# A new written-out order, masks placed by the plan, and one explicit wait between GpSimd and VectorE, in a two-layer linear-attention and GLU kernel

## The chip, the cores and the metric

The kernel runs on one core of one Trainium2 chip. A time is the device time of one execution in microseconds (us), and a kernel's time is the median of several. Engines are named as the profile names them: PE is TensorE (PEld its weight loads), DVE is VectorE, ACT is ScalarE, POOL is GpSimd, SP is SyncE, which here only issues DMAs. A `q` behind an engine's name means its sequencer. "L588" is line 588 of the kernel before; the changed kernel has lines of its own, and what stood at L588 stands there at L621.

## The reference, cut to what matters

The input `x` has 2048 tokens of 512 features in bfloat16. Four residual blocks follow each other; blocks 1 and 3 share one set of weights, and so do blocks 2 and 4.

```python
def _A_ref(x, wqkv, w_phi, wo):          # H = 32 heads of Dh = 16
    q, k, v = split_heads(x @ wqkv)
    pq, pk = q @ w_phi, k @ w_phi        # per head, 16 x 16
    phi_q = concat([softmax(pq), softmax(-pq)])
    phi_k = concat([softmax(pk), softmax(-pk)])
    kv, z = sum_s phi_k^T v, sum_s phi_k # over all 2048 tokens
    return ((phi_q @ kv) / (phi_q . z + 1e-6)) @ wo

def _B_ref(x, W_gate, W_up, W_down):     # F = 1376
    return (relu(x @ W_gate) * (x @ W_up)) @ W_down

x = x + _A_ref(_layernorm(x), ...)
x = x + _B_ref(_layernorm(x), ...)
x = x + _A_ref(_layernorm(x), ...)
x = x + _B_ref(_layernorm(x), ...)
```

`kv` and `z` are sums over all tokens, so no query of a layer can be finished before the last key of that layer has been added.

## The kernel before, in words

The tokens are 16 tiles of 128, and four tiles make a chunk. One layer is a block A and the block B behind it; there are two layers. The functions below do not issue instructions. Each makes operations with an engine, a function that issues the instructions, and the keys that it reads and writes, and puts them into one list, the plan. `Plan.order` then arranges them by the table `ORDER`, one number for each of the 1881 operations, and `Plan.emit` issues them in that order. Each engine executes its own operations in the order of the table and waits where an input is missing. Which engine does an operation that several could do is written in the strings of `STEP` (A is ACT, D is DVE, P is POOL). The numbers given to `pl.op` (durations, earliest times) take no part in the emitted program: `ORDER` alone decides.

The start of the program matters most here. `setup` issues the loads of `x` and the weights (L162), and clears constants. ACT loads its table with a first activation (L172). PE runs 20 dummy matmuls of 128x512 on zeros (L261, `wake`), until work arrives. Then `feature_weights` transposes the key weights, `wkv`, on PE (L294), copies them out (L250 on ACT, L252 on DVE), and folds the 16x16 feature maps into them (L307). For the folding and for the sums at the end of the keys it needs two small masks, `M8` (L198) and `M4` (L200), which DVE makes in `setup`.

LayerNorm of a tile is `BN_STATS` and `BN_AGGR` on DVE (L331, L333), a reciprocal root on POOL (L341), and a scale on ACT, DVE or POOL (L403, L415). The normalised tile is turned by PE (L424, with a copy by ACT or DVE) or by a transposing DMA from SP.

A key tile then takes: four PE matmuls (L653), two exponentials on ACT (L674), sums of exponentials on DVE (L625, L631, L635; for some tiles POOL adds halves first, L622), a reciprocal on DVE (L683), a scaling of the 1024 columns (L688), of which POOL does a first part and DVE the rest as `STEP["ks0"]` says, and PE's sums into `kv` (L711). Value tiles are L606 and their copies L250 or L252. When all 16 key tiles are in, DVE builds `R` from `kv` (L733). Query tiles (L753, L757, ...) can run ahead of that up to the matmul with `R` (L792); DVE divides (L810, L812), PE projects (L843), and DVE adds to `x` (L509). Block B is `glu`: gate and up matmuls (L556), their evictions (L562, L566) and product (L569, L573), the down projection of eleven matmuls a tile (L588), and DVE's addition to `x` (L513). In the last block SP sends each tile out behind that addition (L593); tile 15 goes in three pieces of 256, 128 and 128 columns.

Of the kernel before, what the change touches and what calls it, by code (L numbers as in the profile page):

```python
# [8 lines left out]
P = 128  # L9
D = 512  # L10
# [7 lines left out]
EPS = 1e-5  # L18
# [7 lines left out]
Alu = mybir.AluOpType  # L26
AF = mybir.ActivationFunctionType
AX = mybir.AxisListType
# [22 lines left out]
class Plan:  # L51
# [53 lines left out]
    def emit(self):  # L105
        for o in self.order():
            for b in sorted(o.bufs, key=lambda b: b.kind):
                if b.tile is None:
                    pool, n = self.kinds[b.kind]
                    b.tile = pool.tile(list(b.shape), b.dtype, name=f"{b.kind}{b.slot}", tag=f"{b.kind}{b.slot}", bufs=1)  # L110
            o.fn()

# [4 lines left out]

NV = 8
# [3 lines left out]
WF_IN, WK_IN, WV_IN, WQ_IN, LOADED = 3.5, 5.95, 10.0, 14.1, 13.0  # L122
X_IN = [3.27, 3.85] + [7.2] * 2 + [8.5] * 4 + [11.4] * 4 + [12.8] * 4
TINY = 0.165
# [7 lines left out]
def setup(ctx, tc, A_x, A_wqkv, A_w_phi, A_wo, B_W_gate, B_W_up, B_W_down, out):  # L132
# [32 lines left out]
    for what in LOAD_ACT:  # L165
        load(nc.scalar, what)
# [5 lines left out]
    nc.scalar.activation(out=wake[:], in_=st.zero[:, 0:1], func=AF.Exp)  # L172
    M8f = const.tile([P, 8], F32, name="M8f")
# [24 lines left out]
    nc.vector.tensor_copy(out=M8[:], in_=M8f[:])  # L198
    st.M4 = const.tile([P, 4], BF16, name="M4")
    nc.vector.tensor_reduce(out=st.M4[:], in_=ident[:].rearrange("p (k h) -> p h k", h=4), axis=AX.X, op=Alu.max)  # L200
# [45 lines left out]
def evacuate(st, eng, ends, on_dve, **deps):  # L246

    nc, pl = st.nc, st.pl
    if eng == "A":
        pl.op("ACT", 0.475, lambda: nc.scalar.copy(out=ends()[0], in_=ends()[1]), **deps)  # L250
    else:
        pl.op("DVE", on_dve, lambda: nc.vector.tensor_copy(out=ends()[0], in_=ends()[1]), **deps)  # L252

# [59 lines left out]
class Norm:  # L313
# [8 lines left out]
    def add(self, t):  # L322
# [5 lines left out]
        if self.sums:  # L328
            return self.add_sums(t, n)
        bn = Buf("bnst", [P, 6], F32)  # L330
        pl.op("DVE", 0.597, dur=0.69, fn=lambda: nc.vector.bn_stats(out=bn[:], in_=st.X[:, t, :]), reads=[("X", t)] + ([("Xin", t)] if self.at else []), writes=[(bn, 0)],  # L331
# [448 lines left out]
def attention(st, c, pT, norm, L):  # L780
# [73 lines left out]
    "turn": "AAADDAAD", "wake": 20, "fuse0": "AFAA", "fuse1": "FFFF", "gate": 3, "sA": 3, "xB0": "ADAADDDADDDAAAAA",  # L854
# [5 lines left out]
}  # L860
ORDER = [int(i) for i in """
# [119 lines left out]
def kernel(  # L981
# [4 lines left out]
    with tc.manual_schedule():  # L986
        st.pl.emit()
# [30 lines left out]
```

## Time and profile before

| what | us |
|---|---|
| median of 3 runs | 378.02 (377.85 to 378.4) |
| the profiled execution | 377.86 |
| its span, first to last instruction | 376.1 |
| PE busy | 368.5 |
| DVE busy | 262.5 |
| ACT busy | 212.5 |
| POOL busy | 136.5 |

The profiled execution lies inside the spread of the runs, 0.16 us under their median. Around its span lie 377.86 - 376.1 = 1.76 us. A timeline row reads: start, time until the end of the last instruction in the row, engine, line, operation, what it writes and reads, how many; in brackets the idle time of the engine ahead of it and what ended it. PE's rows overlap, because matmuls are pipelined, so what a matmul costs is the distance between starts.

### The profile page before, as it was taken

What the parts mean: (1) busy time and instruction counts of PE and PEld (TensorE: products, weight loads), DVE (VectorE), ACT (ScalarE), POOL (GpSimd) and SP (SyncE); (2) the same over time, 40 slices, a digit from 0 to 9 for tenths busy, and PEclk for the clock granted to TensorE, in tenths of its full rate; (3) what the DMA queues carried; (4) which work ended last, traced back from release to release, by engine and by line L of the source; (5) the groups of instructions that cost most, each with busy time, mean ns of one, the idle gap of its engine ahead of it and who ended that gap; (6) DMA issues with size and microseconds to landing.
All of it is one profiled execution on the core that took longest, in us unless ns stands there. A gap on an engine that the chain in (4) does not pass through costs nothing.

```text
span 376.1 us, 6927 instructions
## 1 busy us (share of the span) xinstructions
PE 368.5 (98%) x2530; PEld 196.6 (52%) x2530; DVE 262.5 (70%) x608; ACT 212.5 (57%) x478; POOL 136.5 (36%) x223
## 2 busy tenths in 40 slices
PE   8999998999999999999999999999999999999996
PEld 4455445877644545444444446566655454444453
DVE  7999999998879854267554976898875353325343
ACT  4999898767745537784666264786522352042100
POOL 6999998362410028024601765431410011000000
PEclk9999999999999999999999999999999999999999
DMA  8898565675843823400140032266583321000031
GB/s 267 178 194 186 139 147 99 116 108 120 133 93 63 120 43 71 98 0 2 29 92 7 15 58 44 49 121 127 119 136 84 58 62 24 0 14 2 0 110 60
DMA packets 95746, 31.83 MB, mean 85 GB/s; under 512 B 87424, under 2 KB 95200, under 8 KB 95712
## 3 DMA queue, kind: packets, MB, share of 16 engines
q1 hardware_dynamic: 93024, 27.97, 38.4%
q10 hardware_dynamic: 2688, 3.42, 2.7%
q8 instruction: 20, 0.33, 0.4%
q14 instruction: 14, 0.11, 0.1%
HBM read 8.44 MB, written 2.10 MB: 28 GB/s over the span
## 4 chain that ended last, share of the span: by engine, by line
PE 83%; DVE 12%; ACT 1%; DMA 1%; POOL 1%; issue 1%
PE ps L556 37%; PE ps L588 20%; PE ps L843 7%; PE ps L753 4%; PE ps L653 4%; PE ps L536 3%; PE ps L606 3%; DVE b L688 3%; PE q L792 2%; DVE sk L625 2%; DVE rk L683 2%; PE ps L261 1%; DVE sk L635 1%; DMA b<-b 1%; PE q L711 1%; DVE bnst L331 1%
## 5 line engine op out<-in xcount | busy, mean ns | idle before, releaser
L566 ACT ACTIVATE b<-ps 128x512 bf16<-128x512 f32 (+3 forms) x110 | 50.4, 482 | 68.1 <-PE ps L556 67.8
L556 PE MATMUL ps<-b,wu 128*128 128x512 bf16 (+3 forms) x440 | 82.1, 321 | 0.2 <-ACT sq L491 0.2
L556 PE MATMUL ps<-b,wg 128*128 128x512 bf16 (+3 forms) x440 | 81.5, 321 | 0.0
L588 PE MATMUL ps<-wd,b 128*128 128x512 bf16 (+4 forms) x374 | 79.2, 366 | 0.0
L588 PEld LDWEIGHTS <-b 128*128 128x128 bf16 (+1 forms) x374 | 35.3, 98 | 39.3
L556 PEld LDWEIGHTS <-wg 128*128 128x128 bf16 x440 | 38.5, 98 | 31.6
L556 PEld LDWEIGHTS <-wu 128*128 128x128 bf16 x440 | 38.4, 98 | 31.0 <-issue 0.5
L622 POOL TENSOR_TENSOR b<-b 128x256 f32<-128x256 bf16 x39 | 27.5, 718 | 62.8 <-ACT b L757 33.5
L569 DVE SCALAR_TENSOR_TENSOR b<-ps,b 128x512 bf16<-128x512 f32 (+2 forms) x60 | 34.1, 593 | 22.6 <-PE ps L556 12.2
L757 ACT ACTIVATE b<-ps 128x512 bf16<-128x512 f32 x64 | 37.3, 642 | 8.9 <-PE ps L753 7.6
L674 ACT ACTIVATE b<-ps 128x512 bf16<-128x512 f32 x64 | 37.7, 645 | 5.9 <-PE ps L653 5.4
L688 POOL TENSOR_TENSOR b<-b,rk 128x1024 bf16<-128x1024 bf16 (+6 forms) x26 | 36.7, 1424 | 7.5 <-DVE rk L683 4.4
L513 DVE SCALAR_TENSOR_TENSOR X<-ps,r,X 128x512 bf16<-128x512 f32 (+2 forms) x22 | 14.9, 694 | 27.7 <-PE ps L588 27.7
L653 PE MATMUL ps<-Wk,b 128*128 128x512 bf16 x128 | 32.2, 379 | 0.6 <-ACT b L250 0.3
L843 PE MATMUL ps<-wo,b 128*128 128x512 bf16 x128 | 32.7, 379 | 0.0
L753 PE MATMUL ps<-Wq,b 128*128 128x512 bf16 x128 | 32.0, 379 | 0.0
L606 PE MATMUL ps<-wkv,b 128*128 128x512 bf16 x128 | 31.8, 379 | 0.0
L509 DVE SCALAR_TENSOR_TENSOR X<-ps,X 128x512 bf16<-128x512 f32 x32 | 21.7, 679 | 7.4 <-PE ps L843 7.4
L562 ACT ACTIVATE b<-ps 128x128 bf16<-128x128 f32 (+2 forms) x50 | 20.5, 430 | 8.9 <-PE ps L556 8.4
L573 DVE TENSOR_TENSOR b<-b,b 128x128 bf16<-128x128 bf16 (+2 forms) x50 | 15.0, 332 | 14.8 <-ACT b L562 9.8
L773 POOL TENSOR_TENSOR b<-b,rq 128x512 bf16<-128x512 bf16 x21 | 22.1, 1056 | 0.7
L812 DVE TENSOR_TENSOR b<-q,dd 128x512 bf16<-128x512 f32 x32 | 21.8, 683 | 0.6
(94 smaller groups left out, 482.7 us busy)
## 6 DMA issues: line engine op xcount, KB each, us to landing
out_dram<-X SPq DMA_DIRECT2D x15, 128.0 KB, 1.9
X<-in_A_x_dram ACTq DMA_DIRECT2D x3, 512.0 KB, 6.6
b<-b SPq DMA_TRANSPOSE x91, 3.1
wg<-in_B_W_gate_dram SPq DMA_DIRECT2D x8, 160.0 KB, 2.7
wu<-in_B_W_up_dram SPq DMA_DIRECT2D x8, 160.0 KB, 3.2
wd<-in_B_W_down_dram SPq DMA_DIRECT2D x5, 256.0 KB, 3.2
wkv<-in_A_wqkv_dram ACTq DMA_DIRECT2D x2, 512.0 KB, 5.9
wq<-in_A_wqkv_dram ACTq DMA_DIRECT2D x1, 512.0 KB, 4.0
```

Of the source, the lines that this page charges most:

```text
L556: nc.tensor.matmul(ps[:], lhsT=wt[:, b, f * P:(f + 1) * P], rhs=xnT[:, lo:hi, b, :], start=(b == 0), stop=(b == NDB - 1))
L566: pl.op("ACT", 0.045 + 0.43 * share, lambda ups=ups, ru=ru, sign=1.0 if fuse else -1.0: nc.scalar.activation(out=ru[:], in_=ups[:], func=A ...
L569: pl.op("DVE", 0.058 + 0.548 * share, dur=0.138 + 0.548 * share, fn=lambda gps=gps, ru=ru, h=h, cs=cs: nc.vector.scalar_tensor_tensor(out= ...
L588: nc.tensor.matmul(yps[:], lhsT=hs[f][:fsz, ti * P:(ti + 1) * P], rhs=st.wd[:fsz, f, cols], start=(f == 0), stop=(f == NFT - 1))
L606: nc.tensor.matmul(vp[:], lhsT=xnT[:, ti, kb, :], rhs=st.wkv[:, kb, D:2 * D], start=(kb == 0), stop=(kb == NDB - 1))
L622: nc.gpsimd.tensor_tensor(out=h[:].rearrange("p j h f -> p j f h"), in0=x[:, :, 0], in1=x[:, :, 1], op=Alu.add)
L653: nc.tensor.matmul(ps[:], lhsT=xnT[:, ti, kb, :], rhs=w(kb), start=(kb == 0), stop=(kb == NDB - 1))
L674: pl.op("ACT", 0.48, lambda s=s, ek=ek, pk=pk: nc.scalar.activation(out=ek[:, :, s, :], in_=pk[:].rearrange("p (j x) -> p j x", j=8), func ...
L688: eng.tensor_tensor(out=phiK[:, lo:hi, :, :].rearrange("p j s (f h) -> p (j s) f h", h=4), in0=ek[:, lo:hi, :, :].rearrange("p j s (f h) - ...
L753: nc.tensor.matmul(pq[:], lhsT=xnT[:, ti, kb, :], rhs=st.Wq2[:, kb, :], start=(kb == 0), stop=(kb == NDB - 1))
L757: pl.op("ACT", 0.48, lambda s=s, eq=eq, pq=pq: nc.scalar.activation(out=eq[:, :, s, :], in_=pq[:].rearrange("p (j x) -> p j x", j=8), func ...
L843: nc.tensor.matmul(yps[:], lhsT=turned(b), rhs=st.wo[:, b, :], start=(b == 0), stop=(b == NDB - 1))
```

## The change

The list of operations stays the same but for three things: the two masks are operations of the plan now (`masks`), five instead of four value tiles of layer 1 are copied out by DVE, and these are others (`ev1`). A variant of the statistics that would run on ACT is added but not used (`"st"` holds only D). The table `ORDER` is a new one throughout. Two loads of ACT's queue (`x` of tiles 4 to 7, and the value weights) are issued behind the activation that loads ACT's table. The emitter can add a wait: operation 230, POOL's scale of key tile 3, now waits for operation 195, DVE's scale of key tile 0. The constants `WF_IN` to `X_IN` are earliest times for the plan and not part of the program.

```diff
+    def emit(self, tc):
         for o in self.order():
...
             o.fn()
+            o.ins = tc.nc.cur_bb.bb.instructions[-1]
+            for v in BEHIND.get(o.i, ()):
+                tc.add_manual_dep(o.ins, self.ops[v].ins.name, mybir.DependencyInfo(mybir.DependencyClass.Sync, mybir.DependencyReason.ANTI),
[...]
...
+BEHIND = {230: (195,)}
...
-    for what in LOAD_ACT:
+    for what in LOAD_ACT[:3]:
         load(nc.scalar, what)
...
     nc.scalar.activation(out=wake[:], in_=st.zero[:, 0:1], func=AF.Exp)
+    for what in LOAD_ACT[3:]:
+        load(nc.scalar, what)
...
-    nc.vector.tensor_copy(out=M8[:], in_=M8f[:])
     st.M4 = const.tile([P, 4], BF16, name="M4")
-    nc.vector.tensor_reduce(out=st.M4[:], in_=ident[:].rearrange("p (k h) -> p h k", h=4), axis=AX.X, op=Alu.max)
...
+def masks(st):
+
+    nc, pl = st.nc, st.pl
+    pl.rank("w")
+    pl.op("DVE", 0.1, lambda: nc.vector.tensor_copy(out=st.M8[:], in_=st.M8f[:]), writes=[("M8", 0)], at=2.75)
+    pl.op("DVE", 0.17, lambda: nc.vector.tensor_reduce(
+        out=st.M4[:], in_=st.ident[:].rearrange("p (k h) -> p h k", h=4), axis=AX.X, op=Alu.max), reads=[("M8", 0)], writes=[("M4", 0)], at=2.75)
...
-    "xm1": "21121122", "om0": "12222222", "om1": "21221222", "ev0": "AAAAAAAAAAAAAAAA", "ev1": "DAAAAAADAAAAADAD",
...
+    "ev0": "AAAAAAAAAAAAAAAA", "ev1": "AAADADADAAADDAAA", "ks0": "6087060714860850", "ks1": "3484716308718788",
...
 ORDER = [int(i) for i in """
-3 4 5 108 109 110 111 112 113 114 115 116 117 118 7 6 138 8 134 0 9 12 13 14 15 129 128 139 135 16 130 142 131 140
+3 4 5 6 7 14 15 9 8 10 110 111 112 113 114 115 116 117 140 144 136 118 16 17 18 0 132 11 130 131 141 23 145 137 142
```

What the table moves shows in the order of each engine's instructions. The first place is the start on PE. Before, eleven dummy matmuls on `zero` stand ahead of the first transposition of `wkv`; these are the last three of them:

```order
L261 MATMUL ps_140<-zero 128x512
L261 LDWEIGHTS zero
L261 MATMUL ps_142<-zero 128x512
L261 LDWEIGHTS zero
L261 MATMUL ps_144<-zero 128x512
L294 LDWEIGHTS wkv
L294 MATMUL ps_151<-ident,wkv 128x128
```

In the changed kernel these are the seventh and eighth dummy, and the transpositions (now L310) follow:

```order
L277 MATMUL ps_146<-zero 128x512
L277 LDWEIGHTS zero
L277 MATMUL ps_148<-zero 128x512
L310 LDWEIGHTS wkv
L310 MATMUL ps_151<-ident,wkv 128x128
```

Three dummies have moved from ahead of the transpositions to places among them and the foldings behind them.

The second place is POOL around its scale of key tile 3, 128x896 with `rk` of tile 3 as its factor. Before, it stands between two additions of halves (L622):

```order
L341 TENSOR_TENSOR rstd_599<-ve_577,mhalf 128x2
L391 TENSOR_TENSOR ve_613<-u_581,rstd_579 128x2
L391 TENSOR_TENSOR ve_629<-u_568,rstd_599 128x2
L688 TENSOR_TENSOR b_428<-b_427,rk_611 128x896
L622 TENSOR_TENSOR b_704<-b_587 128x8x8x4
L688 TENSOR_TENSOR b_346<-b_345,rk_521 128x1024
```

In the changed kernel the scale of key tile 2, 128x1024, stands directly behind it, and the 128x896 scale is the instruction that got the explicit wait:

```order
L422 TENSOR_SCALAR u_619<-mv_518 128x2
L424 TENSOR_TENSOR ve_621<-u_619,rstd_617 128x2
L721 TENSOR_TENSOR b_441<-b_440,rk_631 128x896
L721 TENSOR_TENSOR b_346<-b_345,rk_509 128x1024
L424 TENSOR_TENSOR ve_689<-u_614,rstd_583 128x2
L655 TENSOR_TENSOR b_691<-b_572 128x8x8x4
```

An addition and one of the small factors of the statistics have moved behind both scales, so POOL now scales twice in a row.

The third place is the end of DVE's program, its additions to `x` in the last block. Before, the last one is a piece of 256 columns of tile 15:

```order
L513 SCALAR_TENSOR_TENSOR X<-ps_5318,r_4853,X 128x512
L513 SCALAR_TENSOR_TENSOR X<-ps_5287,r_4853,X 128x128
L513 SCALAR_TENSOR_TENSOR X<-ps_5334,r_4851,X 128x512
L513 SCALAR_TENSOR_TENSOR X<-ps_5348,r_4853,X 128x512
L513 SCALAR_TENSOR_TENSOR X<-ps_5362,r_4853,X 128x256
```

In the changed kernel the three pieces come earlier and two whole tiles, 8 and 13, close the program:

```order
L546 SCALAR_TENSOR_TENSOR X<-ps_5318,r_4978,X 128x128
L546 SCALAR_TENSOR_TENSOR X<-ps_5332,r_4978,X 128x128
L546 SCALAR_TENSOR_TENSOR X<-ps_5306,r_4978,X 128x256
L546 SCALAR_TENSOR_TENSOR X<-ps_5344,r_4895,X 128x512
L546 SCALAR_TENSOR_TENSOR X<-ps_5362,r_4978,X 128x512
```

The last addition, and the last transfer out behind it, have grown from 256 to 512 columns.

More of the change, by code (lines that the diff above doesn't have):

```diff
@@ L103, in order @@
         return self.seq
-    def emit(self):
+    def emit(self, tc):
         for o in self.order():
@@ L111, in emit @@
             o.fn()
+            o.ins = tc.nc.cur_bb.bb.instructions[-1]
+            for v in BEHIND.get(o.i, ()):
+                tc.add_manual_dep(o.ins, self.ops[v].ins.name, mybir.DependencyInfo(mybir.DependencyClass.Sync, mybir.DependencyReason.ANTI),
+                                  reason="one at a time on the port that VectorE and GpSimd share")
 class KS:
     pass
+BEHIND = {230: (195,)}
 NV = 8
@@ L121 @@
 LATE = ((8, 12), (12, 16), "q")
-WF_IN, WK_IN, WV_IN, WQ_IN, LOADED = 3.5, 5.95, 10.0, 14.1, 13.0
-X_IN = [3.27, 3.85] + [7.2] * 2 + [8.5] * 4 + [11.4] * 4 + [12.8] * 4
+WF_IN, WK_IN, WV_IN, WQ_IN, LOADED = 3.57, 5.83, 10.1, 14.03, 13.0
+X_IN = [3.35, 4.26] + [6.46] * 2 + [8.61] * 4 + [11.37] * 4 + [12.62] * 4
 TINY = 0.165
@@ L329, in add @@
             return self.add_sums(t, n)
+        by_act = self.at is not None and n == 1 and STEP["st"][t] == "A"
+        if by_act:
+            e2, nv, rstd = Buf("u", [P, 4], F32), Buf("ve", [P, 4], F32), Buf("rstd", [P, 4], F32)
+            for out, func, scale in ((lambda: e2[:, 0:1], AF.Square, D ** -0.5), (lambda: mv[:, 0, 0:1], AF.Identity, 1.0 / D)):
+                junk = Buf("sq", [P, D], BF16)
+                pl.op("ACT", 0.67, lambda out=out, func=func, scale=scale, junk=junk: nc.scalar.activation(
+                    out=junk[:], in_=st.X[:, t, :], func=func, scale=scale, accum_out=out()),
+                    reads=[("X", t), ("Xin", t)], writes=[(junk, 0), (e2, 0) if func == AF.Square else (mv, 0)], at=self.at[t])
+            pl.op("POOL", TINY, lambda: nc.gpsimd.tensor_scalar(
+                out=nv[:, 0:1], in0=mv[:, 0, 0:1], scalar1=mv[:, 0, 0:1], scalar2=e2[:, 0:1], op0=Alu.mult, op1=Alu.subtract),
+                reads=[(mv, 0), (e2, 0)], writes=[(nv, 0)])
+            pl.op("POOL", TINY, lambda: nc.gpsimd.tensor_scalar(
+                out=nv[:, 0:1], in0=nv[:, 0:1], scalar1=-1.0, scalar2=EPS, op0=Alu.mult, op1=Alu.add), reads=[(nv, 0)], writes=[(nv, 0), ("stat", t)])
+            pl.op("POOL", 0.39 + 0.155, lambda: nc.gpsimd.tensor_tensor(out=rstd[:, 0:1], in0=nv[:, 0:1], in1=st.mhalf[:, 0:1], op=Alu.pow),
+                  reads=[(nv, 0)], writes=[(rstd, 0)])
+            self.tiles.append(t)
+            return self.normalise(n, mv, rstd)
         bn = Buf("bnst", [P, 6], F32)
-        pl.op("DVE", 0.597, dur=0.69, fn=lambda: nc.vector.bn_stats(out=bn[:], in_=st.X[:, t, :]), reads=[("X", t)] + ([("Xin", t)] if self.at else []), writes=[(bn, 0)],
+        pl.op("DVE", 0.597, dur=0.69, fn=lambda: nc.vector.bn_stats(out=bn[:], in_=st.X[:, t, :]), reads=[("X", t)] + ([("Xin", t), ("M4", 0)] if self.at else []), writes=[(bn, 0)],
               at=self.at[t] if self.at else 0.0)
@@ L853 @@
     "tB0": "A---", "tB1": "---A", "tA": "----", "wev": "DDDAAAAADDDAAAAA", "xn1": "APAPDAADPAAPAAAA",
-    "turn": "AAADDAAD", "wake": 20, "fuse0": "AFAA", "fuse1": "FFFF", "gate": 3, "sA": 3, "xB0": "ADAADDDADDDAAAAA",
[5 rows of a table removed]
+    "st": "DDDDDDDDDDDDDDDD", "turn": "AAADDAAD", "wake": 20, "fuse0": "AFAA", "fuse1": "FFFF", "gate": 3, "sA": 3,
[6 rows of a table added]
 }
 ORDER = [int(i) for i in """
[72 rows of a table removed]
[72 rows of a table added]
 """.split()]
@@ L939, in layers @@
     load_weights(st)
+    masks(st)
     xA = []
@@ L986 @@
     with tc.manual_schedule():
-        st.pl.emit()
+        st.pl.emit(tc)
 _INS = ['A_x', 'A_wqkv', 'A_w_phi', 'A_wo', 'B_x', 'B_W_gate', 'B_W_up', 'B_W_down']
```

151 rows, old and new, of tables (ORDER, STEP) are left out of this document.

## Prediction

> **What bounds the kernel now.** I read the windows first, a table by stage with the busy time (and instructions) of PE, PEld, DVE, ACT and POOL, then PE's clock, the DMAs' share and GB/s, then PE's own waits, then the timelines of the stages in which PE waits.
>
> ```profile
> 20.00:40.00 20.00, 20.00 (x152) 10.42 (x150) 20.00 (x41) 20.00 (x40) 19.62 (x27) 1.00 0.81 174
> 40.00:58.13 18.13, 16.44 (x142) 8.51 (x139) 18.13 (x34) 15.53 (x31) 16.09 (x18) 1.00 0.57 140
> 58.13:212.00 153.87, 153.26 (x1031) 83.20 (x1030) 112.14 (x284) 99.44 (x244) 52.80 (x98) 1.00 0.41 73
> 212.00:262.00 50.00, 49.28 (x455) 28.51 (x454) 40.68 (x95) 31.77 (x71) 23.80 (x33) 1.00 0.40 75
> 262.00:372.90 110.90, 110.90 (x645) 56.28 (x643) 54.33 (x111) 31.29 (x68) 8.53 (x13) 1.00 0.26 56
> ```
>
> From 58 us on PE is the bound: it waits 0.6 us in 154, 0.7 in 50, nothing in the last 111. Its matmuls are the same in both kernels, so a new order can win or lose there only what PE waits. Ahead of 58.13 it is otherwise. That is the start of `R`, and in the 38 us before it DVE is busy without a break, while PE finds 1.7 us of idle time between 40 and 58.
>
> ```profile
> 58.13 0.77 DVE L733 TENSOR_TENSOR R<-M,q 128x272 bf16<-128x272 bf16 x2
> ```
>
> PE's row behind it waits for just that:
>
> ```profile
> 59.04 0.41 PE L792 MATMUL q<-R,b 128*128 128x68 bf16 x8 [0.29 <-DVE R L733]
> ```
>
> So the time is: the moment at which DVE reaches `R`, then PE's work behind it with 1.3 us of waits, then the tail. In both orders the same matmuls stand on PE ahead of its first L792, and on DVE the same operations ahead of L733. What can move the first term is DVE's idle time ahead of `R` and the length of its instructions.
>
> **The start.** DVE's rows up to 18 us show all its idle time of that stage.
>
> ```profile
> 3.38 0.69 DVE L331 BATCH_NORM_STATS2 bnst<-X 128x6 f32<-128x512 bf16 x1 [0.60 <-DMA X<-in_A_x_dram]
> ...
> 5.12 0.25 DVE L200 TENSOR_REDUCE M<-ident 128x4 bf16<-128x128 bf16 x1
> 5.29 0.16 DVE L198 CAST M<-M8f 128x8 bf16<-128x8 f32 x1
> 5.48 0.76 DVE L270 TENSOR_TENSOR Wblk<-M,wf 128x256 bf16<-128x256 bf16 x2
> 6.58 1.18 DVE L252 COPY b<-ps 128x512 bf16<-128x512 bf16 x3 [0.34 <-PE ps L294]
> ...
> 15.62 0.42 DVE L252 COPY b<-ps 128x512 bf16<-128x512 bf16 x1 [0.28 <-PE ps L424]
> ...
> 17.80 0.42 DVE L252 COPY b<-ps 128x512 bf16<-128x512 bf16 x1 [0.24 <-PE ps L424]
> ```
>
> The masks now come ahead of the first `BN_STATS`, into the 0.60 us in which DVE waits for `x`. They held DVE from 5.12 to 5.48, 0.36 us. But the copy at 6.58 already waits 0.34 for PE, and PE cannot turn `wkv` before it has landed, so that wait grows by the same 0.36: the masks alone give nothing at once.
>
> PE's side changes more.
>
> ```profile
> 1.24 4.88 PE L261 MATMUL ps<-zero 128*128 128x512 bf16 x11 [1.24 <-DVE zero L170]
> 5.91 1.61 PE L294 MATMUL ps<-ident,wkv 128*128 128x128 bf16 x16
> ...
> 7.58 0.59 PE L261 MATMUL ps<-zero 128*128 128x512 bf16 x2
> 8.01 0.83 PE L307 MATMUL ps<-Wblk,b 128*128 128x128 bf16 x12
> ```
>
> ```profile
> 5.86 1.25 PEld L294 LDWEIGHTS <-wkv 128*128 128x128 bf16 x12 [0.66 <-DMA wkv<-in_A_wqkv_dram]
> ```
>
> Eleven dummies take 5.91 - 1.24 = 4.67 us, 0.425 each; two later ones take 8.01 - 7.58 = 0.43, 0.215 each. PE starts at half speed (the PEclk column shows 1.00 throughout and misses this). Sixteen transpositions take 1.44 us; at 0.215 / 4 and twice that a column block costs 0.054 and 0.107, so about eleven were slow and the step came near 5.91 + 11 x 0.107 = 7.1 us, after 5.8 us of unbroken work. With eight dummies PE is done at 1.24 + 8 x 0.425 = 4.64 and idles 1.2 us until `wkv` lands at 5.86. If the idle time does not matter, the step stays at 7.1. If PE must again be busy for 5.8 us, it comes at 11.7. I take 10.5, nearer to the only stretch that the rows show. [...]
>
> With the step at 10.5, 3.4 us more pass at half speed, and PE falls back by 1.7 us. DVE needs PE's turned tiles at the two copies quoted at 15.62 and 17.80, and there it has no slack now. In the new order it has some: tile 3's copy stands behind one more `BN_STATS` (0.59 us to the next start) and PE turns that tile 0.25 earlier, tile 4's turn stands 1.1 earlier on PE and its copy 0.3 earlier on DVE, so both have about 0.8. DVE then stalls 1.7 - 0.8 = 0.9, less the 0.28 + 0.24 that it waits there now: +0.4. ACT starts its exponentials late by as much; the sums of key tile 4 and 6 have under 1 us of slack to them, and I add 0.2. **Head: +0.6 us**. Without the delay both stalls vanish, -0.5; with the step at 11.7 the lag is 2.3 and the head +1.2.
>
> **The scales.** On DVE, the length of an L688 scale depends on what POOL does.
>
> ```profile
> 27.77 0.28 DVE L688 TENSOR_TENSOR b<-b,rk 128x256 bf16<-128x256 bf16 x1
> ...
> 28.75 0.62 DVE L688 TENSOR_TENSOR b<-b,rk 128x1024 bf16<-128x1024 bf16 x1
> ...
> 31.42 2.54 DVE L688 TENSOR_TENSOR b<-b,rk 128x1024 bf16<-128x1024 bf16 x2
> ```
>
> POOL's rows of the same stretch:
>
> ```profile
> 31.04 1.69 POOL L688 TENSOR_TENSOR b<-b,rk 128x896 bf16<-128x896 bf16 x1
> 32.70 1.12 POOL L622 TENSOR_TENSOR b<-b 128x256 f32<-128x256 bf16 x1
> 33.77 1.96 POOL L688 TENSOR_TENSOR b<-b,rk 128x1024 bf16<-128x1024 bf16 x1
> ```
>
> The 1024-wide scale alone takes 0.62 us and the 256-wide one 0.28; the pair begun inside POOL's scale of tile 3 takes 2.54, 1.6 more. So a DVE scale that meets a POOL scale can lose up to what is left of it, 1.7 to 2.0 us. In the new order other pairs meet: the scale of key tile 4 falls where POOL adds, tiles 7, 8 and 9 fall into POOL's scale of tile 7. I find some gained and some lost and take 0, with -1.2 to +1.2 as bounds, about one long collision either way.
>
> **The explicit wait** is for DVE's scales of key tiles 1 and 0, 0.62 + 0.28 us behind the reciprocal for which POOL's scale waits anyway.
>
> ```profile
> 28.30 0.54 DVE L683 RECIPROCAL rk<-sk 128x64 bf16<-128x64 f32 x1
> ```
>
> That reciprocal ends at 28.84 now and POOL starts at 31.04, 2.2 us later, because its own queue holds it; the work ahead of it on POOL stays within 0.2 us. 0.9 fits into 2.2: cost 0, at most 0.9. If POOL came early, the scale of tile 2 (1.96), additions for `sk` and `sq`, and behind them PE's sums L711 would wait too. The table load moved ahead of two loads costs nothing: the row below shows an issue during it.
>
> ```profile
> 3.63 1.28 ACT L172 ACT_TABLE_LOAD   x1 [3.63 <-issue]
> 3.70 0.47 ACTq L162 DMA_DIRECT2D X<-in_A_x_dram  x1
> ```
>
> The last load of `x` is now issued behind an ACT copy of PE's transpositions, some 0.7 us later than the 5.99 of before; its tiles 12 to 15 are first used at 18.14, so this is covered.
>
> **Layer 2's start.** PE waits for a transposition once.
>
> ```profile
> 224.49 1.04 PE L653 MATMUL ps<-Wk,b 128*128 128x512 bf16 x4 [0.23 <-DMA b<-b]
> ```
>
> In the new order the four last down projections of layer 1 follow each other, with the value matmuls behind them, so the chain from the last of them starts 1.9 us of PE work earlier. That can take away this wait and the gap around it, 0.4 us from start to start; DVE has one more copy of a value tile there (0.66), in a stretch in which it is busy 40.7 of 50 us. **I take -0.2**, between -0.4 and a new wait of +0.4.
>
> **The tail.** The last rows of DVE, and the transfers out with the time to their landing:
>
> ```profile
> 372.01 0.75 DVE L513 SCALAR_TENSOR_TENSOR X<-ps,r,X 128x512 bf16<-128x512 f32 x1 [1.63 <-PE ps L588]
> 373.21 0.48 DVE L513 SCALAR_TENSOR_TENSOR X<-ps,r,X 128x256 bf16<-128x256 f32 x1 [0.46 <-PE ps L588]
> ```
>
> ```profile
> out_dram<-X SPq DMA_DIRECT2D x11, 128.0 KB, 1.8
> out_dram<-X SPq DMA_DIRECT2D x2, 32.0 KB, 1.5
> out_dram<-X SPq DMA_DIRECT2D x1, 64.0 KB, 1.5
> ```
>
> PE ends with the same total of work, but what follows its last matmul is an addition over 512 columns instead of 256, 0.75 - 0.48 = 0.27, and a transfer of 128 KB instead of 64 KB, 1.8 - 1.5 = 0.3. Nothing hides the end. **Tail: +0.55 us**, between 0.27 and 0.9 (the slowest landing of a transfer out).
>
> **Sum.** +0.6 + 0 + 0 - 0.2 + 0.55 = +0.95. The profiled execution took 377.86 us with a span of 376.1; it would take 378.8. Put on the median of the runs, which is 0.16 above it, this is 378.02 + 0.95 = **379.0 us**.
>
> **Rivals.** First, the cover holds: the stretch at half speed does not grow, DVE's two stalls go, -0.5, one collision of scales less, -0.6, the wait of layer 2 goes, -0.4; with the tail +0.55 the sum is -0.95, 377.1, and 376.5 at the far bound of the scales, -1.2. For it speaks that PE was busy 3.4 us before its pause, against it that this had not raised its speed. Second, PE's lag is covered but nothing is won: 0 at the head, tail +0.55, layer 2 -0.2, 378.4, within the bound. [...] Last, the explicit wait may do nothing, since it is met before POOL gets there; this holds in every case above, and is why it has no term.
>
> **How the numbers follow.** About 0.2%, 0.76 us, is what a measurement of this kernel can tell from no change. My forecast, 378.2 to 379.8 around 379.0, gets 0.38, of which 0.10 lies within 0.2%. The rival that is faster gets 0.28 (0.22 beyond 0.2%), the covered one 0.16, the collisions 0.18. So faster 0.22, same 0.10 + 0.06 + 0.16 = 0.32, slower 0.28 + 0.18 = 0.46. The range of 376.7 to 381.0 leaves out a third of the first outer case and half of the last, 0.18.
>
> **What would show it.** The start on PE: eight dummies, a pause of 1.2 us, and where the distance of two dummies falls from 0.43 to 0.215 us; at 7.1 my head is wrong. [...] The last addition on DVE should take 0.75. If PE's idle time between 58 and 372 has grown by more than 1 us, I have missed a wait that the new order makes where PE is the bound.

## The result, and the profile after

The changed kernel takes 377.37 us (median of 12 runs, 376.99 to 377.72), the kernel before 378.14 in the same comparison (12 runs). The ratio is 0.998, with an interval of 0.9973 to 0.9988: faster by 0.5 to 1.0 us, where a slower one was forecast. The profiled execution took 377.40 us with a span of 375.7, against 377.86 and 376.1.

Three moments cut the span into the terms of the prediction: PE's first matmul on `R`, DVE's last addition to `x`, and the end. In the changed kernel PE's and DVE's timelines have these rows:

```profile
59.11 0.41 PE L825 MATMUL q<-R,b 128*128 128x68 bf16 x8
```

```profile
372.31 0.75 DVE L546 SCALAR_TENSOR_TENSOR X<-ps,r,X 128x512 bf16<-128x512 f32 x1 [1.63 <-PE ps L621]
```

| stretch | before, us | after, us | measured | forecast |
|---|---|---|---|---|
| head: start to the first matmul on `R` | 59.04 | 59.11 | +0.07 | +0.6 |
| body: from there to the last addition | 373.21 - 59.04 = 314.17 | 372.31 - 59.11 = 313.20 | -0.97 | -0.2 |
| tail: from there to the end of the span | 376.1 - 373.21 = 2.89 | 375.7 - 372.31 = 3.39 | +0.50 | +0.55 |
| sum | | | -0.40 | +0.95 |

**The head** comes out even, but not because nothing happened. DVE's rows of waiting for PE, ahead of the same copies as before, have grown:

```profile
6.60 0.42 DVE L259 COPY b<-ps 128x512 bf16<-128x512 bf16 x1 [0.77 <-PE ps L310]
...
16.84 0.42 DVE L259 COPY b<-ps 128x512 bf16<-128x512 bf16 x1 [0.77 <-PE ps L457]
...
18.36 0.42 DVE L259 COPY b<-ps 128x512 bf16<-128x512 bf16 x1 [0.51 <-PE ps L457]
```

They are 2.05 us now and were 0.34 + 0.28 + 0.24 = 0.86. On PE's timeline the reason is seen:

```profile
5.95 1.46 PE L310 MATMUL ps<-ident,wkv 128*128 128x128 bf16 x12 [1.12 <-DMA wkv<-in_A_wqkv_dram]
7.21 0.63 PE L277 MATMUL ps<-zero 128*128 128x512 bf16 x1
...
9.34 0.63 PE L277 MATMUL ps<-zero 128*128 128x512 bf16 x1
9.77 0.43 PE L323 MATMUL ps<-Wblk,b 128*128 128x128 bf16 x4
10.03 0.38 PE L277 MATMUL ps<-zero 128*128 128x512 bf16 x1
```

The dummies at 7.21 and 9.34 are followed after 0.42 and 0.43 us by the next row, the one at 10.03 after 0.21 (the next row, not shown, starts at 10.24). So the step to full speed fell near 9.8 us, behind the pause, as the forecast had it (10.5). The trace also records when the full clock was granted, here from 9.84 us on.

What paid for this is the second half of the head. The groups of DVE's scales up to 58.13 us, by shape (busy time, then mean ns of one); first before, then after:

```profile
L688 DVE TENSOR_TENSOR b<-b,rk 128x1024 bf16<-128x1024 bf16 x5 | 5.2, 1041 | 0.0
...
L688 DVE TENSOR_TENSOR b<-b,rk 128x128 bf16<-128x128 bf16 x2 | 0.6, 289 | 0.0
```

```profile
L721 DVE TENSOR_TENSOR b<-b,rk 128x1024 bf16<-128x1024 bf16 x5 | 3.3, 654 | 0.0
L721 DVE TENSOR_TENSOR b<-b,rk 128x128 bf16<-128x128 bf16 x2 | 2.2, 1096 | 0.0
```

And all thirteen together, before and after:

```profile
L688 DVE TENSOR_TENSOR b<-b,rk 128x1024 bf16<-128x1024 bf16 (+5 forms) x13 | 10.3, 807 | 0.0
```

```profile
L721 DVE TENSOR_TENSOR b<-b,rk 128x1024 bf16<-128x1024 bf16 (+5 forms) x13 | 8.8, 709 | 0.0
```

The busy times differ by 1.5 us, but records of neighbouring scales overlap in them. Thirteen times the means, and the distances from start to next start, give 1.3 us less. The five wide ones run near the 0.62 us of one that nothing disturbs. The three of 256 columns, of which two began inside additions of POOL before, take 0.75 us less together:

```profile
L688 DVE TENSOR_TENSOR b<-b,rk 128x256 bf16<-128x256 bf16 x3 | 1.8, 594 | 0.0
```

```profile
L721 DVE TENSOR_TENSOR b<-b,rk 128x256 bf16<-128x256 bf16 x3 | 1.0, 345 | 0.0
```

The two small ones of 128 columns now take 0.96 and 1.23 us, 1.6 us more together, because both begin inside a scale of POOL. The first of them, and POOL's two scales:

```profile
31.82 0.96 DVE L721 TENSOR_TENSOR b<-b,rk 128x128 bf16<-128x128 bf16 x1
```

```profile
31.01 3.57 POOL L721 TENSOR_TENSOR b<-b,rk 128x896 bf16<-128x896 bf16 x2
```

**The body.** All that PE waits for between 58 and 372 us, before and after:

```profile
PE ps L832 <- DVE b L812: 0.3, 1, 0.3
PE q L792 <- DVE b L812: 0.3, 1, 0.3
PE q L792 <- DVE R L733: 0.3, 1, 0.3
PE ps L653 <- DMA b<-b: 0.2, 1, 0.2
PE ps L556 <- ACT sq L491: 0.2, 1, 0.2
```

```profile
PE ps L865 <- ACT b L790: 0.3, 1, 0.3
PE q L825 <- DVE b L845: 0.3, 1, 0.3
```

The wait of 0.3 us for `R` lies ahead of the first matmul on `R`, in the head. The two waits of 0.2 us are gone. Counted from start to start of matmuls, less what such a matmul costs elsewhere, they were gaps of 0.39 us near 224 and 0.32 near 253; three of 0.07 to 0.09 us between 68 and 79, which the list is too coarse for, have gone too.

**The tail** did what was said: the last addition takes 0.75 us, and the transfers out of 128 KB in the last stretch need

```profile
out_dram<-X SPq DMA_DIRECT2D x3, 128.0 KB, 1.8
```

1.8 us to land, where the 64 KB piece needed 1.5.

### The profile page after: what moved, and what is told of

It is laid out like the page before. It is cut to its first block, busy times and chain, and to the rows that moved or that the text cites. A ratio compares the mean times of both kernels' runs of the same rounds, so it can differ in the third digit from the quotient of the medians.

```text
span 375.7 us, 6932 instructions
## 1 busy us (share of the span) xinstructions
PE 368.1 (98%) x2530; PEld 197.2 (52%) x2530; DVE 264.0 (70%) x609; ACT 211.4 (56%) x477; POOL 136.4 (36%) x223
## 4 chain that ended last, share of the span: by engine, by line
PE 87%; POOL 6%; DVE 5%; DMA 1%; issue 0%; ACT 0%; ACTq 0%
PE ps L589 37%; PE ps L621 20%; PE ps L876 7%; PE ps L786 5%; PE ps L686 4%; PE ps L639 4%; PE ps L569 3%; PE q L825 2%; POOL b L721 2%; POOL b L655 2%; PE q L744 1%; DMA wkv<-in_A_wqkv_dram 1%; POOL b L448 1%; DVE b L721 1%; DVE rk L716 1%; PE ps L277 1%
## 5 line engine op out<-in xcount | busy, mean ns | idle before, releaser
L621 PE MATMUL ps<-wd,b 128*128 128x512 bf16 (+3 forms) x374 | 79.2, 366 | 0.0
L655 POOL TENSOR_TENSOR b<-b 128x256 f32<-128x256 bf16 x39 | 26.3, 687 | 50.9 <-ACT b L790 31.6
L790 ACT ACTIVATE b<-ps 128x512 bf16<-128x512 f32 x64 | 36.2, 616 | 7.6 <-PE ps L786 5.8
L721 POOL TENSOR_TENSOR b<-b,rk 128x1024 bf16<-128x1024 bf16 (+6 forms) x26 | 37.7, 1461 | 7.0 <-DVE rk L716 7.0
L707 ACT ACTIVATE b<-ps 128x512 bf16<-128x512 f32 x64 | 36.8, 629 | 4.9 <-PE ps L686 4.7
L257 ACT CAST vext<-ps 128x512 bf16<-128x512 f32 x27 | 16.2, 620 | 12.7 <-PE ps L639 12.7
L524 ACT ACTIVATE sq<-b 128x512 bf16<-128x512 bf16 x32 | 20.2, 632 | 4.2 <-DVE b L503 4.1
```

The lines of the kernel that those rows point to most:

```text
L621: nc.tensor.matmul(yps[:], lhsT=hs[f][:fsz, ti * P:(ti + 1) * P], rhs=st.wd[:fsz, f, cols], start=(f == 0), stop=(f == NFT - 1))
L655: nc.gpsimd.tensor_tensor(out=h[:].rearrange("p j h f -> p j f h"), in0=x[:, :, 0], in1=x[:, :, 1], op=Alu.add)
L707: pl.op("ACT", 0.48, lambda s=s, ek=ek, pk=pk: nc.scalar.activation(out=ek[:, :, s, :], in_=pk[:].rearrange("p (j x) -> p j x", j=8), func ...
L721: eng.tensor_tensor(out=phiK[:, lo:hi, :, :].rearrange("p j s (f h) -> p (j s) f h", h=4), in0=ek[:, lo:hi, :, :].rearrange("p j s (f h) - ...
L790: pl.op("ACT", 0.48, lambda s=s, eq=eq, pq=pq: nc.scalar.activation(out=eq[:, :, s, :], in_=pq[:].rearrange("p (j x) -> p j x", j=8), func ...
```

## The experiments

Each was compared with the kernel before on the same chip. Some are hybrids of the two orders, which are easy to make: of the operations ahead of `R` of layer 1 only nine stand on different sides of it in the two tables, and of those ahead of `R` of layer 2 one. Besides the times, the table at the end of this section has the three stretches of every profile.

**1. Without the explicit wait** (`a_nowait`)

```diff
-BEHIND = {230: (195,)}
+BEHIND = {}
```

> The changed kernel without its explicit wait; the order is untouched. Theory (the wait is met before GpSimd gets to the scale of key tile 3): the scale starts at 31.0 us as in the changed kernel, VectorE's R starts within 0.1 us of 58.18, and the time stays about 0.8 us under the kernel before (ratio 0.998). Rival (the wait keeps the two engines' scales apart, and the shorter scales on VectorE, 8.8 instead of 10.3 us in 13, come from it): without it that sum goes back towards 10.3, R comes 1 us or more later, near 59.3, and the time is at or above the kernel before.

Measured: 377.75 us, ratio 0.9991 (0.9982 to 1.0). POOL's timeline shows no idle time ahead of the scale, with the wait gone:

```profile
31.21 0.20 POOL L424 TENSOR_TENSOR ve<-u,rstd 128x2 f32<-128x2 f32 x1
31.36 3.57 POOL L721 TENSOR_TENSOR b<-b,rk 128x896 bf16<-128x896 bf16 x2
```

The thirteen scales take 8.8 us as in the changed kernel, so the rival, which put the shorter scales down to the wait, falls. `R` comes 0.35 us later, and so does POOL's scale; in this profile the step to full speed came at 10.6 us instead of 9.8, and DVE's waits for PE are 2.52 us instead of 2.05. The wait is met when POOL gets there: in the changed kernel DVE's scale of tile 0 ends by 29.99, POOL begins at 31.01. The time itself doesn't settle it: its interval meets that of the changed kernel.

**2. Eleven dummies ahead again** (`a_eleven`), in `ORDER`:

```diff
-110 111 112 113 114 115 116 117 140 144 136 118
+110 111 112 113 114 115 116 117 118 119 120 140 144 136
```

(119 and 120 are taken out where they stood, further on)

> The changed kernel with eleven dummy matmuls ahead of the first transposition, as before, instead of eight. Theory (the pause on PE delays the step to full speed, and the delay costs VectorE): the distance of 512-column matmuls falls to 0.215 us near 7.1 us instead of 9.9; VectorE's waits for PE ahead of its copies shrink from 2.0 us to about 0.9; R starts 0.6 to 0.9 us earlier, near 57.4, and the time is 0.6 to 0.9 us under that of the changed kernel (1.4 to 1.7 under the kernel before). Rival 1 (the speed of PE at the start is covered further on, or the scales fall into each other in another way when VectorE comes earlier): R stays within 0.3 us of 58.18. Rival 2 (the step comes at about 10 us however PE is used before): the rows of the start do not change.

Measured: 377.11 us, ratio 0.9974 (0.9965 to 0.9983). DVE's timeline:

```profile
17.18 0.42 DVE L259 COPY b<-ps 128x512 bf16<-128x512 bf16 x1 [0.20 <-PE ps L457]
...
26.47 0.42 DVE L664 TENSOR_REDUCE sk<-b 128x32 f32<-128x256 f32 x1 [0.58 <-POOL b L655]
...
57.98 0.79 DVE L766 TENSOR_TENSOR R<-M,q 128x272 bf16<-128x272 bf16 x2
```

The step came at 6.0 us and the waits for PE shrank from 2.05 to 1.1 us, as the theory had it, but `R` gained 0.2 and not 0.6 to 0.9, with the first tile of `x` landing at the same time (3.5 us). DVE arrives 0.9 us earlier at the sums and waits there 0.58 for an addition by POOL, whose queue had not become faster. Rival 1 holds: most of the delay at the start is covered further on.

**3. The old order up to `R`, the new one behind it** (`h_head`; `ORDER` is the first 421 entries of the old table in the new numbers, with the two masks ahead, then the rest of the new table; `BEHIND` is empty)

> The operations of the changed kernel; up to R of layer 1 in the order of the kernel before, from there in that of the changed kernel, and no explicit wait. Theory (the gain lies behind R, in waits of PE at the end of layer 1, at the start of layer 2 and in between, and the head is worth nothing): R starts within 0.2 us of 58.13 and the time is within 0.3 us of the changed kernel, 0.5 to 1.0 us under the kernel before. Rival (the head of the new order also makes the gain possible, by what it leaves in the queues): the waits behind R come back and the time is within 0.2% of the kernel before.

Measured: 377.58 us, ratio 0.9986 (0.9976 to 0.9995), 0.7 us under the kernel before in the medians. First matmul on `R` at 59.00, body 313.21 us, to 0.01 that of the changed kernel. The gain is made behind `R`, with either head ahead of it.

**4. The new order, but the old one from `R` to `R`** (`h_mid`, made in the same way)

> The changed kernel, but from R of layer 1 to R of layer 2 its operations stand in the order of the kernel before; behind that the new order again. Theory (the middle holds about 0.5 us of the gain): PE's waits near 224 us (0.39) and near 78 us (0.24) come back, and the time is 0.4 to 0.7 us above the changed kernel, 0.1 to 0.4 under the kernel before. Rival (the gain lies in the last block, where 0.32 us of waiting at 253 us went): within 0.15 us of the changed kernel.

Measured: 378.46 us, ratio 1.0007 (0.9997 to 1.0018), body 314.25, 1.05 above that of the changed kernel and more than expected. The profile shows a wait of PE near 223 us (0.4) for a value tile that DVE copies out: the old order does not suit the new choice of DVE's value tiles. So this run is no clean removal, and it was repeated with the old choice.

**5. The same with the old choice of value tiles** (`h_mid2`)

```diff
-    "ev1": "AAADADADAAADDAAA"
+    "ev1": "DAAAAAADAAAAADAD"
```

> As the previous exchange of the middle (from R of layer 1 to R of layer 2 in the order of the kernel before, the rest as in the changed kernel), but with the kernel before's choice of the value tiles that VectorE copies out in layer 2, so that no wait of PE for such a copy is added by the mixture itself. Theory (the new order of the middle gains 0.4 to 0.7 us, mostly at PE's wait near 224 us for a turned tile): this wait of 0.4 us comes back, PE's way from R of layer 1 to R of layer 2 is 0.5 to 0.7 us longer than in the changed kernel, and the time lies 0.4 to 0.8 us above it, near 377.9. Rival (the gain comes from the other tiles that VectorE copies): the way is as long as in the changed kernel.

Measured: 377.76 us, ratio 0.9984 (0.9974 to 0.9995); body 313.80, 0.60 above the changed kernel, within what the theory gave. But not by the wait it named: PE does not wait near 224 us. It waits near 252, which the theory had not expected of this part of the order:

```profile
251.96 0.42 PE L825 MATMUL q<-R,b 128*128 128x68 bf16 x8
252.60 2.11 PE L589 MATMUL ps<-b,wu 128*128 128x384 bf16 x12 [0.22 <-DMA b<-b]
```

From start to start that gap is 0.38 us; the other 0.2 lies in gaps of 0.05 to 0.14 near 68 to 70 us. The middle of the order is worth about 0.6 of the 0.97; which of its waits appears depends on more than that.

**6. The old end behind the new middle** (`h_end`)

> The changed kernel up to R of layer 2, and from there the order of the kernel before. Theory (the waits of PE behind the first R go because of the order ahead of the second R, and the new end costs 0.5 us): from the first matmul on R to the last addition 313.2 to 313.4 us (313.20 in the changed kernel, 314.17 before), no wait near 253 us, 2.9 us from the last addition to the end of the span as before (3.39 in the changed kernel), and a time 0.3 to 0.6 us under the changed kernel, near 376.9. Rival (the wait near 253 us belongs to the order behind R of layer 2): 0.3 us of waiting there is back, and the time is within 0.2 us of the changed kernel.

Measured: 377.17 us, ratio 0.9962 (0.9948 to 0.9976). Tail 2.86, 0.53 less than in the changed kernel, as the theory had it. Body 313.39, with a gap of 0.22 near 253 us: a part of that wait belongs to the old end. The theory is right in the size of the tail and only partly on that wait.

**7. Eleven dummies and a small last piece** (`a_eleven_tail`; the last entries of `ORDER`, tile 13, tile 8, then tile 15 in 256, 128, 128 columns):

```diff
-1874 1877 1878 1879 1880 1806 1881 1882 1875 1876 1807 1808 1868 1869 1870
+1868 1869 1870 1806 1807 1808 1874 1875 1876 1877 1878 1879 1880 1881 1882
```

> The changed kernel with eleven dummies ahead of the first transposition and another end: tiles 13 and 8 first, then tile 15 in its pieces of 256, 128 and 128 columns. Theory (what follows PE's last matmul is one addition and one transfer out, and both shrink): the time from PE's last matmul to the end falls from 3.8 us to 3.1 to 3.4, and the time is 0.4 to 0.7 us under that of the kernel with eleven dummies alone, near 376.5. Rival (the landing does not depend on the size, or SP's issues stand in a row): under 0.2 us.

Measured: 376.81 us, ratio 0.9958 (0.9943 to 0.9974).

```profile
373.01 0.35 DVE L546 SCALAR_TENSOR_TENSOR X<-ps,r,X 128x128 bf16<-128x128 f32 x1 [0.27 <-PE ps L621]
```

From this addition to the end of the span (375.7) are 2.69 us, 0.70 less than in the changed kernel. In the profiled execution the first tile of `x` landed 0.3 us later than in that of the changed kernel and `wkv` 1.2 us later, and `R` started at 58.68, so its whole time says less than its tail.

**8. The old order with eight dummies** (`b_eight`)

```diff
-108 109 110 111 112 113 114 115 116 117 118 7 6 138 8 134 0
+108 109 110 111 112 113 114 115 7 6 138 8 134 0
```

(the other three stand behind the third and fourth transposition and the first folding)

> The kernel before with one thing changed: eight dummies ahead of the first transposition, the other three among transpositions and foldings as in the changed kernel. Theory (the pause puts the step to full speed off by about 3 us, and the old order has no slack for it): the step falls between 9.5 and 11 us, VectorE waits 1 to 2 us more for PE ahead of 20 us, R starts 0.8 to 1.6 us later than 58.13, and the time is 0.7 to 1.5 us above the kernel before. Rival (VectorE's waits are taken back by shorter scales later on, as it looks in the changed kernel): R within 0.3 us of 58.13, the time unchanged.

Measured: 379.41 us, ratio 1.0018 (1.0003 to 1.0033), but in two groups: five runs of 377.84 to 378.53 and seven of 379.39 to 379.87. The profiled one was of the lower (377.89); in it PE works at full speed from its first transposition at 6.1 us on, and `R` starts at 57.95. The trace records the full clock from 5.2 us on, while PE's last dummy began at 4.2. So in this execution the step came during the pause. That was in no theory.

**9 to 11. No dummies ahead, and the changed kernel once more** (`a_none`, `b_none`, `after2`). The first two leave out the first 8 and 11 dummies, in the changed kernel thus:

```diff
-nc.tensor.matmul(z[:], ...)
+(lambda: None) if i < 8 else lambda z=z: nc.tensor.matmul(z[:], ...)
```

> The changed kernel without its first eight dummy matmuls, so that PE's first work is the transposition of wkv at 5.9 us. Theory (the step to full speed comes at a time that differs between executions, and comes late in all of them if PE has not worked before its pause; the new order has room for most of such a delay): the step falls at 9.3 us or later in every execution, R starts 0 to 0.7 us later than 58.18, and the time is 377.4 to 378.2, in one group. Rival (a late step costs the new order as much as the old): 1.2 to 1.6 us more than the changed kernel, 378.6 to 379.0.

> The kernel before without its first eleven dummy matmuls. Theory (the two groups of times of the kernel before with eight dummies, 377.8 to 378.5 and 379.4 to 379.9, are an early and a late step): without dummies the step is late in every execution, so all times lie in or above the upper group, 379.4 to 380.5, and R starts 1.2 us or more after 58.13. Rival (the groups have another cause): the times stay near 378, or stay in two groups.

> The changed kernel as it is, once more, beside the two kernels without leading dummies. Theory (the step comes before PE's pause or after it, by chance, and the new order pays only 0.3 to 0.7 us for the late one): a median of 377.2 to 377.6, spread over at most 0.8 us and not in two groups 1.5 us apart; if the profile shows the step near 4.2 us, R starts near 57.9, and if it shows it near 10 us, near 58.2 to 58.5. Rival (the step is tied to PE's work and not to chance): the step falls within 0.2 us of 9.9 again.

Measured for the changed kernel once more: 377.63 us (377.05 to 378.20), ratio 0.9977 (0.9966 to 0.9987), which confirms the result. Its profile shows another start than the first:

```profile
6.18 0.84 PE L310 MATMUL ps<-ident,wkv 128*128 128x128 bf16 x12 [1.52 <-DMA wkv<-in_A_wqkv_dram]
6.86 0.38 PE L277 MATMUL ps<-zero 128*128 128x512 bf16 x1
```

Twelve transpositions take 0.84 us instead of 1.46: PE is at full speed from 6.2 us on, and the trace records the full clock from 4.4 us on, ahead of the pause. DVE's waits for PE are 1.27 us, it waits 0.57 for POOL at 26.24, and `R` starts at 57.73. The fourth dummy starts at 2.49 us in both profiles, and the step came at 4.4 us here and at 9.8 there: it is not tied to PE's work alone, and the rival falls.

Without dummies the changed kernel takes 379.02 us (377.83 to 379.63), ratio 1.0015 (1.0006 to 1.0024): the theory's 377.4 to 378.2 is wrong. In the profiled execution, the fastest of its runs, the step came at 9.9 us and `R` at 58.24. The old order without dummies takes 378.81 us (378.05 to 380.84), ratio 1.0021 (1.0007 to 1.0034), and not one group above 379.4. Its profile (378.75) has the step at 10.3 us, and DVE's rows

```profile
17.14 0.43 DVE L252 COPY b<-ps 128x512 bf16<-128x512 bf16 x1 [1.49 <-PE ps L424]
```

```profile
59.10 0.76 DVE L733 TENSOR_TENSOR R<-M,q 128x272 bf16<-128x272 bf16 x2
```

So a late step costs both orders, and the new one is no shelter from it: only where the profiles show a step near 10 us does the new order look better (58.24 against 59.10 for `R`, with `x` landing 0.2 us later in the better one), and that is one execution of each.

**12. POOL's scale behind its additions** (`a_best`: number 7, and in `ORDER` operation 194, POOL's scale of key tile 0, moved behind 226 and 225, its next two additions)

> As the kernel with eleven dummies and the smaller end, and GpSimd's scale of key tile 0 (768 columns) stands behind its next two additions of halves instead of ahead of them. Theory (with eleven dummies it is GpSimd's queue that holds VectorE, 0.58 us near 26.5, because the scale stands ahead of the additions): this wait goes, R comes 0.4 to 0.6 us earlier than with eleven dummies alone, near 57.5, and the time falls by as much, to about 376.0. [...]

Measured: 376.93 us (376.34 to 377.10), ratio 0.996 (0.9946 to 0.9974). DVE's wait at 26.5 is gone. But the wide scales, by shape as above, take longer again:

```profile
L721 DVE TENSOR_TENSOR b<-b,rk 128x1024 bf16<-128x1024 bf16 x5 | 5.0, 1010 | 0.0
```

The mean hides that four of the five stay between 0.62 and 0.73 us and one takes 2.40. This one begins at 32.43, just behind the start of the second of POOL's two scales:

```profile
30.67 3.61 POOL L721 TENSOR_TENSOR b<-b,rk 128x896 bf16<-128x896 bf16 x2
```

All thirteen take 9.6 us instead of 8.8, and `R` starts at 57.81, 0.17 earlier than in number 2, but `x` had landed 0.23 earlier. So what the wait gave, 0.58 us, the collisions took. The run shows how directly the scales' lengths hang on POOL's queue: one POOL operation of 1.5 us stands behind two others, nothing else changed in the head, and another pair of scales falls together. This kernel and number 7, whose intervals overlap, beat the kernel before by 1.2 to 1.4 us. Their intervals just overlap that of the changed kernel, so that they beat it too is likely and not shown.

| kernel | full speed from | `R` starts | body | tail | median |
|---|---|---|---|---|---|
| before | 7.1 | 58.13 | 314.17 | 2.89 | 378.14 |
| changed | 9.8 | 58.18 | 313.20 | 3.39 | 377.37 |
| changed, once more | 4.4 | 57.73 | 313.40 | 3.34 | 377.63 |
| 1, no wait | 10.6 | 58.53 | 313.19 | 3.35 | 377.75 |
| 2, eleven dummies | 6.0 | 57.98 | 313.21 | 3.38 | 377.11 |
| 3, old head | 7.0 | 58.09 | 313.21 | 3.39 | 377.58 |
| 4, old middle | 10.1 | 58.24 | 314.25 | 3.38 | 378.46 |
| 5, old middle, old value tiles | 5.5 | 57.87 | 313.80 | 3.40 | 377.76 |
| 6, old end | 10.5 | 58.81 | 313.39 | 2.86 | 377.17 |
| 7, small last piece | 5.7 | 58.68 | 313.40 | 2.69 | 376.81 |
| 8, old order, eight dummies | 5.2 | 57.95 | 314.39 | 2.84 | 379.41 |
| 9, new order, no dummies ahead | 9.9 | 58.24 | 313.47 | 3.35 | 379.02 |
| 10, old order, no dummies ahead | 10.3 | 59.10 | 314.11 | 2.87 | 378.81 |
| 12, POOL's scale moved | 4.2 | 57.81 | 313.21 | 2.65 | 376.93 |

The stretches are those of one execution each; a median is of all runs. "Full speed from" is where the trace's record of the full clock begins; in every profile the distances of PE's matmuls agree with it.

## Why the prediction was wrong, step by step

**The body is the step that failed most: "I take -0.2, between -0.4 and a new wait of +0.4".** It measured -0.97. The windows in the prediction had all of PE's idle time behind `R`, 0.6 and 0.7 us, and the sum took up one wait of it, at layer 2's start. That wait went entirely (0.4). The one near 253 us (0.32) and the small gaps near 70 and 80 (0.25) were not priced at all, though a wholly new order is as free to remove them. Experiment 3 shows that this is where the gain is made: with the old head the body has the same 313.21 us. Experiments 5 and 6 put about 0.6 of it on the order between the two `R` and 0.2 on the end. That the four down projections in a row remove the wait at 224 us is not shown: with the old middle it did not come back.

**The scales: "I find some gained and some lost and take 0, with -1.2 to +1.2 as bounds".** They measured -1.3 us, just outside the bounds. What a DVE scale loses is, as the prediction says, what is left of POOL's instruction when it starts, but the prediction did not add this up over the new order. Before, nine of the thirteen started inside a scale or an addition of POOL, with 5.8 us of POOL's instructions left in sum; in the changed kernel six do, with 4.1 us left. Additions count too: before, the scale of 256 columns at 33.21 took 0.75 us instead of 0.28, with 0.61 us of an addition left. Collisions, to which the prediction gave 0.18, have the right place and the wrong sign: into the pair of POOL scales in a row (POOL's 3.57 us from 31.01) fall a scale of 128 columns and one of 256, the other of 128 falls into POOL's scale at 39.13, and none of the five wide ones takes much over its 0.62 us (654 ns on the mean). No run shows the +1.2 us of collisions that the upper end of the range, 381.0, takes in: the thirteen scales took 8.8 to 10.3 us in all fourteen profiles, the longest being those of the kernel before.

**The late step: "+0.6 us".** In the profiled execution the step came at 9.8 us and DVE's waits for PE grew by 1.19 us, of which 0.43 stand in the place of the masks (0.36), as the prediction had said of them. So +0.76 at the two later copies, where it had +0.4; the +0.2 for ACT's lag no run shows by itself. The size is about right; that the step is late in every execution is wrong, and why the profiled one was a late one is not shown. In `after2` the same kernel had its step at 4.4 us. Nor does the step need the 5.8 us of unbroken work that the prediction read from the trace before: in number 12 it came at 4.2 us, 3.0 us after PE's first dummy. Six profiles have this head with eight dummies, one of them without the explicit wait. Counted from the landing of `x` (the start of the first `BN_STATS`), `R` starts after 54.46 and 54.47 us in the two with an early step (`after2` and number 5) and after 54.70 to 55.23 us in the four with a late one (the changed kernel, numbers 1, 4 and 6): a late step costs 0.2 to 0.8 us. The three profiles of the old head with dummies ahead (before, numbers 3 and 8) lie at 54.65 to 54.79. Without the late step the waits for POOL at 26 us (0.57) come in their place.

So the head's +0.07 is a sum of larger terms: waits for PE +1.19, masks -0.36, the first landing of `x` +0.1, scales -1.3, and +0.4 in many small pieces of DVE's timeline, such as its twenty reciprocals (0.2) and its sixteen `BN_STATS` (0.1).

**The tail: "+0.55 us".** It measured +0.50, and experiments 6 and 7 take 0.53 and 0.70 away again. Right.

**What was costed at nothing**: the explicit wait, right by experiment 1; the table load ahead of two loads was not tried by itself, and no engine's wait in the head names either of the two.

What stays open: what makes the step early or late; which condition brings the waits near 224 and 253 us; what separates the two groups of experiment 8, since only the lower one was profiled (an early and a late step would fit), and the spread of experiments 9 and 10, since a late step alone would have put experiment 10 above 379.4; and why the whole time gained 0.77 us in the medians and 0.46 in the profiled executions. The early or late step moves `R` by as much as that difference, but which runs had which is not recorded.

## What to carry to other kernels

When a whole order is replaced, price every wait of the bounding engine that the trace lists, and the gaps between starts that the list is too coarse for, not the one wait that a visible move explains: each may go, and together they gave 0.97 us where 0.2 was taken. A length of an instruction that depends on another engine's queue is to be added up instruction by instruction: what is left of POOL's where DVE's begins, whatever the width of DVE's (5.8 us in sum before, 4.1 in the changed kernel). Put the smallest piece last: 0.53 to 0.74 us at the end of this kernel, in the profile of every run that tried it.

## What the runs showed of the hardware

At the start the distance of two matmuls of 512 columns on PE is 0.425 us, and from a step on 0.215. This step to full speed comes at different times in executions of one program: at 4.4 us and at 9.8 in the changed kernel, and, with an unchanged first 4.6 us of dummies, between 4.2 and 10.6 in its variants. Pauses of 0.6 us (number 12), 1.2 us (number 7) and 1.5 us (`after2`) between dummies and transpositions did not bring the slow speed back where the step had come before them. The recorded stretch of full clock lasts 368.64 us in the trace of the kernel before, from 7.06 us on, and 365.23 us in that of the changed kernel, from 9.84 on.

In the seven profiles with eight dummies ahead (the changed kernel twice, numbers 1, 4, 5, 6 and 8) the step came between 4.4 and 5.5 us in three and between 9.8 and 10.6 in four. In the five with eleven (before, numbers 2, 3, 7 and 12) it came between 4.2 and 7.1, in the two without dummies at 9.9 and 10.3. So the late steps with eight lie 2.7 us or more behind every step with eleven. What decides between early and late these runs do not show: these are fourteen executions, and none could choose it.

A scale on DVE that begins inside a scale of POOL took longer by nearly all that is left of POOL's, narrow or wide. One of 128 columns took 0.15 us alone; the two in the changed kernel took 0.81 and 1.08 us more, with 0.88 and 1.15 us left. One of 1024 took 0.62 us alone; the one at 31.42 us before took 1.25 more with 1.32 left, and the one in number 12 took 1.78 more with 1.85 left. The least share is that of one of 256 columns at 34.25 in the changed kernel, 0.20 more with 0.33 left.
